# Storing the last 128-token tile of an attention and feed-forward kernel in two DMAs per half instead of four

## The chip, the core and the metric

The kernel runs on one core of a Trainium2 chip. The metric is the device time of one execution in microseconds (us). Before the change it is 646.36 us, the median of 3 runs, which lie between 646.31 and 646.38.

A core has five engines with instruction streams of their own: TensorE (PE, with its weight loads as PEld), VectorE (DVE), ScalarE (ACT), GpSimd (POOL) and SyncE (SP). SP and ACT also start DMAs, each on a hardware queue of its own; the profile calls the issuing instructions SPq and ACTq and the two queues q1 (SP's) and q10 (ACT's). Both queues are served by the same 16 DMA engines. A DMA moves its data in packets, here one packet for each run of contiguous bytes, and reports its end with packets of 4 bytes that count up a semaphore.

## The reference

Eight batches of eight heads with 576 tokens of 64 dimensions go through an attention over 32 memory slots per head. The result, 4608 tokens by 512, goes through a two-layer network with a leaky activation.

```python
a = softmax(phi)                                   # 8, 8, 576, 32
k_m = einsum('bhsm,bhsd->bhmd', a, k)
v_m = einsum('bhsm,bhsd->bhmd', a, v)
x = softmax(q @ k_m.T / 8) @ v_m                   # to (4608, 512)
h = x @ w_in                                       # 512 -> 2048
return maximum(0.01 * h, h) @ w_out                # 2048 -> 512, float32
```

## The kernel before

The order of all work is written out by hand: two long strings of step names (`OPENING`, `LATER`) are run one after the other, and no scheduler moves an instruction. The feed-forward part works on groups of tokens. A group from number 3 on takes 256 tokens, and the last group (number 16) only the 128 that are left, all from the last batch.

For that last group the product with `w_out` is accumulated in two halves of 256 output columns, in two PSUM tiles (`po`). `down_tile` (L1542) issues the matmuls: steps `d55.0` to `d55.3` finish half 0, then comes `end.0`, then `d55.4` to `d55.7` finish half 1, and `end.1` is the last step of the program. Both `end` steps are `store_half`: it scales the finished half into `obs` (half 0 on ACT at L1379, half 1 on DVE at L1377) and sends it to `out` in DRAM.

The tokens of a batch stand permuted in the kernel: column `32 * j + x` of a batch is token `18 * x + j`. The last 128 columns are `j` = 14 to 17 with `x` = 0 to 31. So 32 partitions of `obs` hold one `j`, and go to 32 rows of `out` that lie 18 rows (36 KB) apart, in each a run of 256 floats (1 KB). `store_half` sends one `j` per DMA: `y` = 0 and 2 on SP's queue, 1 and 3 on ACT's. `send` (L1366) does the same for whole rows of the other groups, all on SP.

Each DMA gets one of eight semaphores in turn, `DMAHW0` to `DMAHW7`, and waits until the DMA that had it before has ended. After the last step, SP waits at the end of the program (L1698) for every semaphore, and a barrier of all engines closes the execution.

Of the kernel before, what the change touches and what calls it, by code (L numbers as in the profile page):

```python
# [186 lines left out]
def kernel(  # L187
# [41 lines left out]
    nc = tc.nc  # L229
# [4 lines left out]
    P = 128  # L234
# [1097 lines left out]
    def columns(G, t):  # L1332

        if G < G2:
            for x in range(t * P, (t + 1) * P, 32):
                b, tb = blocks(G)[x // SB]
                y = x % SB // 32
                if b == 0:
                    j = y // 2 * 2 + x // SB if G == 0 else NJ + (0, 2, 1)[y // 2]
                    yield b, j * D + y % 2 * 32  # L1340
                else:
                    yield b, tb * SB + y * 32
        else:
            x0 = 2 * S + (G - G2) * 2 * HT + t * P
            for x in range(x0, x0 + P, 32):
                yield x // S, x % S

    def row_scale(G, t):
        bs = [b for b, _ in columns(G, t)]
        if G == 0:  # L1350
            return 1.0 / WT
        if bs[0] == bs[-1]:
            return osc[:, bs[0]:bs[0] + 1]
        return osc_t[:, bs[0] // 2:bs[0] // 2 + 1]
# [18 lines left out]
    def store_half(G, h, po):  # L1373

        ob, cs = obs[:, h * E:h * E + EH], slice(h * EH, (h + 1) * EH)
        if h:
            nc.vector.tensor_scalar_mul(ob, po[:, 0:EH], row_scale(G, 0))  # L1377
        else:
            nc.scalar.activation(ob, po[:, 0:EH], AF.Copy, scale=row_scale(G, 0))  # L1379
        rows = out.rearrange("(b x j) e -> b j x e", b=B, j=JT)  # L1380
        b, x0 = next(columns(G, 0))
        for y in range(P // 32):
            eng = nc.scalar if y % 2 else nc.sync
            eng.dma_start(rows[b, x0 // 32 + y, :, cs], ob[32 * y:32 * y + 32])

    pos = {}

# [272 lines left out]
    for h in range(2):  # L1660
        steps[f"end.{h}"] = lambda h=h: store_half(G, h, pos[G][h])
# [41 lines left out]
```

## Time and profile before

| | |
|---|---|
| median of 3 runs | 646.36 us (646.31 to 646.38) |
| span of the profiled execution, first to last instruction | 643.4 us |
| median less that span | 2.96 us |
| PE busy | 634.6 us, 99% of the span |
| DVE, ACT busy | 513.4 us, 394.2 us |
| TensorE's clock as granted | full speed in all 40 slices |
| DMA, mean | 95 GB/s |
| stores of the last tile (L1384) | 4 DMAs of 32 KB on SP's queue, 4 on ACT's |

The times are those of one profiled execution, in us from the start of its span. The profile has no device time of its own for that execution, so the 2.96 us between its span and the median of the runs are taken as lying outside the span and as fixed.

### The profile page before, as it was taken

The page shows a single profiled execution, that of the slowest core. Times are in us where ns is not written, and L with a number is a line of the kernel's source. Part 1 is how long each engine was busy: PE and PEld are TensorE (multiplying, and loading weights), DVE is VectorE, ACT ScalarE, POOL GpSimd, SP SyncE. Part 2 cuts the span into 40 slices and gives each one's busy share as a digit, 9 for nine tenths or more (in the row PEclk, how much of TensorE's full clock was granted, in tenths as well). Part 3 has the DMA queues.
Part 4 walks back from the last instruction along what each step waited for, and adds up shares of the span by engine and source line. Part 5 has one row for each costly group of instructions (what it writes and reads, how often), then busy time and mean ns, then how long its engine had stood idle before and what let it go on. Part 6 is the DMA issues. An engine that isn't in the chain of part 4 may idle for free.

```text
span 643.4 us, 16918 instructions
## 1 busy us (share of the span) xinstructions
PE 634.6 (99%) x7149; PEld 481.7 (75%) x7149; DVE 513.4 (80%) x861; ACT 394.2 (61%) x683; POOL 30.0 (5%) x46
## 2 busy tenths in 40 slices
PE   8999999999999999999999999999999999999997
PEld 4545445665546788888888888888888888889896
DVE  5776899998987899899879966799887897574641
ACT  3898987764554556467556665655574576565553
POOL 0000121000010001002000010000010001000000
PEclk9999999999999999999999999999999999999999
DMA  9998632214602645422272001254114101010102
GB/s 323 345 382 274 240 111 54 79 27 86 197 10 36 135 148 85 133 78 42 34 171 91 21 13 44 39 108 148 37 31 80 23 18 34 2 34 2 34 2 50
DMA packets 85884, 61.15 MB, mean 95 GB/s; under 512 B 62128, under 2 KB 69040, under 8 KB 85808
## 3 DMA queue, kind: packets, MB, share of 16 engines
q1 hardware_dynamic: 85328, 59.64, 33.0%
q8 instruction: 56, 0.92, 0.6%
q10 hardware_dynamic: 480, 0.43, 0.2%
q14 instruction: 20, 0.16, 0.1%
HBM read 50.59 MB, written 9.45 MB: 93 GB/s over the span
## 4 chain that ended last, share of the span: by engine, by line
PE 93%; DMA 4%; ACT 1%; DVE 1%; issue 0%; SPq 0%; ACTq 0%
PE po L1507 32%; PE ph L1439 22%; PE po L1396 15%; PE ph L1309 8%; PE ph L1507 5%; PE pa L1217 4%; PE pa L774 3%; DMA arena<-in_moe_w_in_dram 2%; PE po L1542 1%; PE pa L1024 1%; DMA arena<-in_moe_w_out_dram 1%; DMA wo<-in_k_dram 1%; ACT wi L424 0%; PE pa L357 0%; SPq L389 0%
## 5 line engine op out<-in xcount | busy, mean ns | idle before, releaser
L1507 PEld LDWEIGHTS <-arena 128*128 128x128 f16 x2184 | 209.7, 98 | 32.0 <-issue 8.6
L1455 ACT ACTIVATE wi<-ph,g_sc 128x256 f32<-128x256 f32 (+1 forms) x224 | 98.8, 464 | 161.3 <-PE ph L1439 154.3
L1439 PE MATMUL ph<-a,w_mem 128*128 128x256 f16 (+3 forms) x1440 | 144.9, 246 | 0.0
L1439 PEld LDWEIGHTS <-w_mem 128*128 128x128 f16 x1440 | 114.4, 98 | 13.9 <-issue 2.9
L1507 PE MATMUL po<-wo,arena 128*128 128x256 f16 x936 | 122.1, 273 | 0.0
L1507 PE MATMUL po<-arena 128*128 128x256 f16 x936 | 122.1, 273 | 0.0
L1396 PE MATMUL po<-wo,arena 128*128 128x512 f16 (+1 forms) x384 | 110.3, 434 | 0.0
L1484 DVE TENSOR_TENSOR arena<-arena 128x1024 f16<-128x1024 f32 x52 | 63.6, 1222 | 20.6 <-ACT arena L1480 20.6
L1484 DVE TENSOR_TENSOR arena<-wi,arena 128x768 f16<-128x768 f32 (+1 forms) x60 | 54.7, 911 | 10.1 <-ACT arena L1480 10.1
L1476 DVE TENSOR_TENSOR arena<-wi 128x256 f32<-128x256 f32 x104 | 40.4, 430 | 25.9 <-ACT wi L1455 25.3
L1480 ACT CAST arena<-arena 128x1024 f16<-128x1024 f32 x52 | 54.4, 1046 | 8.6 <-DVE arena L1476 8.5
L1309 PE MATMUL ph<-a,w_mem 128*128 128x192 f16 (+2 forms) x304 | 52.1, 317 | 0.0
L1396 PEld LDWEIGHTS <-arena 128*128 128x128 f16 x288 | 27.8, 98 | 29.7 <-issue 0.6
L1480 ACT CAST arena<-wi 128x768 f16<-128x768 f32 (+1 forms) x60 | 46.5, 776 | 1.5
L1476 DVE TENSOR_TENSOR arena<-wi,arena 128x256 f32<-128x256 f32 x104 | 45.7, 440 | 1.8
L1507 PE MATMUL ph<-wo,arena 128*128 128x256 f16 x312 | 42.6, 273 | 0.0
L1182 POOL TENSOR_TENSOR a<-t,a 128x128 f16<-128x128 f32 (+3 forms) x17 | 21.7, 1297 | 444.9 <-ACT a L1177 444.9
L1396 PEld LDWEIGHTS po<-wo,arena 128*128 128x128 f32 x96 | 17.7, 191 | 20.4 <-issue 17.6
L1217 PE MATMUL pa<-wi,vT 64*32 64x512 f16 (+1 forms) x704 | 29.4, 420 | 0.2 <-DVE t L1098 0.2
L1309 PEld LDWEIGHTS <-w_mem 128*128 128x128 f16 x240 | 20.8, 98 | 10.6 <-issue 3.9
L1316 ACT ACTIVATE arena<-ph,g_sc 128x384 f32<-128x384 f32 x32 | 18.3, 579 | 16.1 <-PE ph L1309 15.8
L1250 ACT ACTIVATE w_mem<-pa 128x512 f16<-128x512 f32 x40 | 22.7, 596 | 8.4 <-PE pa L1217 7.4
(233 smaller groups left out, 759.2 us busy)
## 6 DMA issues: line engine op xcount, KB each, us to landing
out_dram<-obs SPq DMA_DIRECT2D x140, 64.0 KB, 1.7
arena<-in_k_dram SPq DMA_DIRECT2D x28, 288.0 KB, 4.4
arena<-in_v_dram SPq DMA_DIRECT2D x28, 288.0 KB, 4.7
arena<-in_q_dram SPq DMA_DIRECT2D x96, 72.0 KB, 2.9
arena<-in_moe_w_in_dram SPq DMA_DIRECT2D x12, 512.0 KB, 7.4
arena<-in_moe_w_out_dram SPq DMA_DIRECT2D x8, 768.0 KB, 7.9
arena<-in_phi_dram SPq DMA_DIRECT2D x7, 576.0 KB, 4.7
arena<-in_moe_w_in_dram SPq DMA_DIRECT2D x8, 256.0 KB, 6.2
```

The lines of the kernel that those rows point to most:

```text
L774: nc.tensor.matmul(var["pk"][g][hh * M:(hh + 1) * M, cs], ld["phi"][rows, hh, j, :], ld["kv", hh][rows, kinds[0]:kinds[-1] + 1, j, :], sta ...
L1182: nc.gpsimd.tensor_tensor(piece(lo, tb), piece(t2, tb), piece(hi, tb), ALU.subtract)
L1217: nc.tensor.matmul(pf[g][cols, :], lhs, rhs, start=(n == 0), stop=(n == len(passes) - 1), tile_position=(g * D, hh * M),)
L1250: nc.scalar.activation(tiles(halves(w16(b, j), g)[:, 0]), w(g), AF.Copy, scale=ws)
L1309: nc.tensor.matmul(ph[:, t0:t0 + n * SB], lhs, rhs, start=(m == 0), stop=(m == len(seq) - 1))
L1396: nc.tensor.matmul(po, lhs, rhs, start=(f == 0 and m == 0), stop=(f == NQ * NF - 1 and m == len(seq) - 1),)
L1439: nc.tensor.matmul(ph[:, t0:t0 + n], lhs, rhs, start=(m == 0), stop=(m == len(seq) - 1))
L1455: nc.scalar.activation(dst, ph, AF.Prelu, scale=g_sc2[:, j:j + 1], alpha=SLOPE)
L1476: nc.vector.tensor_tensor(gt[:, x], y, z, op)
L1480: nc.scalar.copy(dst[:, 0], src)
L1484: nc.vector.tensor_tensor(dst[:, 1], src, dst[:, 0], ALU.subtract)
L1507: nc.tensor.matmul(acc, g[:, x, s, u], rhs, start=(h == 0 and j == 0 and u == 0 and m == 0), stop=(j == NQ - 1 and u == 1 and m == 2), ski ...
```

## The change

`store_half` sends two neighbouring `j` in one DMA. The loop over `y` takes steps of two, the source is 64 partitions of `obs`, and the target is a pattern with two dimensions of rows: 2 values of `j` outside, 32 of `x` inside. SP's queue gets `j` = 14 and 15, ACT's 16 and 17.

```diff
         b, x0 = next(columns(G, 0))
-        for y in range(P // 32):
-            eng = nc.scalar if y % 2 else nc.sync
-            eng.dma_start(rows[b, x0 // 32 + y, :, cs], ob[32 * y:32 * y + 32])
+        for y in range(0, P // 32, 2):
+            eng = nc.scalar if y else nc.sync
+            j = x0 // 32 + y
+            eng.dma_start(rows[b, j:j + 2, :, cs], ob[32 * y:32 * y + 64])
```

On SP the end of the program reads as follows, before (-) and after (+). `obs` is the tile of scaled results, `32x256` and `2x32x256` are rows by elements at the target in DRAM.

```order
 L1366 DMA out_dram<-obs 32x512 [waits DMAHW1_49]
 L1366 DMA out_dram<-obs 32x512 [waits DMAHW2_49]
-L1384 DMA out_dram<-obs 32x256 [waits DMAHW4_49,Activation_49]
-L1384 DMA out_dram<-obs 32x256 [waits DMAHW5_49]
-L1384 DMA out_dram<-obs 32x256 [waits DMAHW7_49,DVE_49]
-L1384 DMA out_dram<-obs 32x256 [waits DMAHW1_49]
-L1698 UNCONDITIONAL_BRANCH
+L1385 DMA out_dram<-obs 2x32x256 [waits DMAHW4_49,Activation_49]
+L1385 DMA out_dram<-obs 2x32x256 [waits DMAHW6_49,DVE_49]
+L1699 UNCONDITIONAL_BRANCH
```

SP issues two DMAs fewer; its second store now waits for DVE's scaling, as the third did before.

On ACT the last rows of the program before are these.

```order
L1379 ACTIVATE obs<-po,osc 128x256 [waits DMAHW2_49,DMAHW1_49,DMAHW7_49,DMAHW0_49,PE_49]
L1384 DMA out_dram<-obs 32x256 [waits DMAHW3_49,Activation_49]
L1384 DMA out_dram<-obs 32x256 [waits DMAHW6_49]
L1384 DMA out_dram<-obs 32x256 [waits DVE_49]
L1384 DMA out_dram<-obs 32x256
```

After the change the same place holds these.

```order
L1379 ACTIVATE obs<-po,osc 128x256 [waits DMAHW2_49,DMAHW1_49,DMAHW7_49,DMAHW0_49,PE_49]
L1385 DMA out_dram<-obs 2x32x256 [waits DMAHW3_49,Activation_49]
L1385 DMA out_dram<-obs 2x32x256 [waits DMAHW5_49,DVE_49]
```

ACT too issues two DMAs fewer, and nothing on any engine stands in another order than before.

## Rows read from the trace of the kernel before

**Rows 1.** The page: busy time of PE, and the chain that ended last by engine.
```profile
PE 634.6 (99%) x7149; PEld 481.7 (75%) x7149; DVE 513.4 (80%) x861; ACT 394.2 (61%) x683; POOL 30.0 (5%) x46
...
PE 93%; DMA 4%; ACT 1%; DVE 1%; issue 0%; SPq 0%; ACTq 0%
```

**Rows 2.** The chain in order of time, its last pieces: start, us, what.
```profile
633.33 5.91 PE po L1542 x54
639.24 0.03 issue
639.26 0.48 DVE obs L1377
```

**Rows 3.** Timeline, four short windows at the end: start, us, engine, line, what.
```profile
637.96 0.47 ACT L1379 ACTIVATE obs<-po,osc 128x256 f32<-128x256 f32 x1 [3.78 <-PE po L1542]
...
638.45 0.31 SPq L1384 DMA_DIRECT2D out_dram<-obs  x1
638.46 0.38 ACTq L1384 DMA_DIRECT2D out_dram<-obs  x1
...
639.77 0.31 SPq L1384 DMA_DIRECT2D out_dram<-obs  x1
639.78 0.37 ACTq L1384 DMA_DIRECT2D out_dram<-obs  x1
...
640.13 0.42 SPq L1384 DMA_DIRECT2D out_dram<-obs  x1
640.18 0.44 ACTq L1384 DMA_DIRECT2D out_dram<-obs  x1
```

**Rows 4.** DMA issues at 639.77 and 639.78: KB, us from issue to landing.
```profile
out_dram<-obs SPq DMA_DIRECT2D x1, 32.0 KB, 1.4
out_dram<-obs ACTq DMA_DIRECT2D x1, 32.0 KB, 1.6
```

**Rows 5.** DMA issue at 640.18: KB, us from issue to landing.
```profile
out_dram<-obs ACTq DMA_DIRECT2D x1, 32.0 KB, 1.7
```

**Rows 6.** SP's waits at the program's end: ns min/median/max, first and last start.
```profile
L1698 SPq EVENT_SEMAPHORE  x7: 17/28/1329, 640.6 to 643.3; - x7
```

**Rows 7.** DMA activity from 638.4 to 641.9 in 40 slices of 0.0875 us.
```profile
DMA  0000000002588414686200000587613687200000
...
DMA packets 384, 0.26 MB, mean 75 GB/s; under 512 B 128, under 2 KB 384, under 8 KB 384
...
q1 hardware_dynamic: 192, 0.13, 14.7%
```

**Rows 8.** Issue times by line: ns min/median/max, first and last start.
```profile
L1384 SPq DMA_DIRECT2D out_dram<-obs x4: 314/368/422, 638.5 to 640.1; - x4
...
L664 SPq DMA_DIRECT2D r1k<-d_mx x12: 487/554/2362, 116.9 to 464.7; - x12
...
L601 SPq DMA_DIRECT2D arena<-in_q_dram x96: 565/630/1811, 138.8 to 497.1; - x96
```

**Rows 9.** Two DMAs of 64 rows: timeline, then DMA activity from 222.4 in slices of 0.05 us.
```profile
222.45 1.13 SPq L664 DMA_DIRECT2D r1k<-d_mx  x2
...
DMA  0000000000000000000000000029333222221213
```

**Rows 10.** SP's DMA queue from 138 to 156: packets; then the DMAs issued there.
```profile
q1 hardware_dynamic: 10000, 1.77, 52.5%
...
arena<-in_q_dram SPq DMA_DIRECT2D x16, 72.0 KB, 2.9
arena<-in_phi_dram SPq DMA_DIRECT2D x1, 576.0 KB, 4.2
```

**Rows 11.** Busy time from 8 to 18 us, with the DMA engines' share and rate at the end.
```profile
core 0: us, PE busy (x) PEld busy (x) DVE busy (x) ACT busy (x) POOL busy (x), PEclk, DMA share, GB/s
8.00:18.00 10.00, 8.63 (x127) 5.52 (x128) 6.92 (x19) 6.14 (x13) 0.00 (x0) 1.00 1.04 388
```

## The prediction

> **What bounds the kernel now.** I read the page first: PE is busy for 99% of the span and the chain that ended last is PE's for 93% [rows 1]. The stores of the last tile are none of that, except at the very end. So I went to the chain in order of time. Its last piece of PE ends at 639.24, DVE scales half 1 until 639.74, and there the chain of engines stops [rows 2]; the span goes on to 643.4. What fills those 3.7 us is in the timeline: half 1 is issued in two rounds on both queues, at 639.77 and 639.78, then at 640.13 and 640.18 [rows 3]. The last of the four lands 1.7 us after 640.18, at about 641.9 [rows 5]. That it is this landing which is waited for shows at the program's end: SP's longest wait starts at 640.6 and takes 1.33, so it ends at 641.93 [rows 6]. The remaining 1.47 us are the closing barrier and stay. Only a change of 641.93 counts.
>
> Half 0 is off the path today. Its DMAs go out at 638.45 and 638.46 and 0.4 later [rows 3], and the activity of the DMA engines shows them over well before half 1 begins: one burst from slice 9 to slice 19 (639.2 to 640.1), then nothing, then half 1 from slice 25 to slice 34 (640.6 to 641.46) [rows 7]. From the last data at 641.46 to 641.93 pass 0.47 us, the landing of the last write.
>
> **What is removed.** The second issue on each queue, which today starts 0.36 to 0.40 after the first [rows 3]. The first DMAs of half 1 land after 1.4 and 1.6 [rows 4], so if nothing else changed, the end would be set by ACT's issue at 639.78.
>
> **What is added: a dearer form.** The new DMAs have 64 partitions on one side and 2 by 32 rows on the other. The plain stores of 32 rows take 0.31 to 0.42 to issue on SP. Two other lines of this program are dearer: L664, with 64 rows of 1 KB, at 0.49 at least and 0.55 in the median, and L601, whose target is 32 partitions of 18 runs while its source is one list of 576, at 0.63 in the median [rows 8]. L601 is the only one with a different number of dimensions on its two sides, like the new store. Between 64 runs and 576 the issue grows by 0.08 in the median, so it is paid for the form and not for the runs. From L664's issue at 222.45 to the first activity (slice 26, 223.70 or a little after) pass 1.28 us [rows 9]; for today's stores it is 639.25 less 638.45, or 0.80 [rows 3, 7]. Bounds for issue to first packet: 0.80, if the form costs nothing, and 1.42, L664's with the 0.14 that L601 takes longer to issue than L664's shortest. I take L664's 1.28, nearest in bytes and rows. So half 0's first packet goes from 639.25 to 639.73.
>
> **What is added: fewer DMA engines, perhaps.** Today each of the eight DMAs writes 16 packets of 4 bytes beside its 32 packets of data: 384 packets, of which 128 are small [rows 7]. So each is shared by all 16 engines, two rows for each. The same holds for every form I could count: from 138 to 156 SP's queue carries sixteen L601 DMAs and one of phi (128 partitions by 4 runs), and 16 x 576 + 512 packets of data leave 272 of the 10000, which is 17 x 16 [rows 10]. With 18 and 4 as inner counts, the share can't be cut along the inner dimension, since 16 divides neither; it follows the outer one (576 and 32, 128 and 128), or the flat list of runs. The new store is the first DMA whose outer count on one side isn't a multiple of 16: it is 2. If the share follows the outer counts, two engines get 32 rows each. And both queues' DMAs go to the same two, if engines are counted from the first. [...]
>
> [...]
>
> **The sum for two engines.** Half 0 brings 32 packets from SP's queue and 32 from ACT's to each of the two engines, half 1 as many: 128 packets of 1 KB each, one after the other. Half 1 is issued at 639.77, its packets are ready by 641.05 (1.28 later), and half 0 is not through by then, so the engines don't pause. The price of a packet lies between two rows. When all engines are saturated with long rows, 388 GB/s over 16 engines at a share of 1.04 is 23.3 GB/s for one, or 44 ns for 1 KB [rows 11]. In today's tail, 14.7% of 16 engines over 3.5 us is 8.23 us for 128 rows on q1, small packets included, so at most 64 ns [rows 7]; there 16 engines at once read the same 32 partitions. Two engines alone are nearer to the first; I take 48. Then 128 x 48 is 6.14 us, from 639.73 to 645.87, and with 0.47 for the landing 646.34. That is 4.41 later than 641.93. On the profiled execution it gives a span of 647.8, and with the 2.96 between span and median 650.8.
>
> Half 0, free today because it ends before half 1 begins, now stands in front of it: that is 3.07 of the 4.41. Bounds: 639.25 + 128 x 44 + 0.47 = 645.35, or 649.8; and 639.87 + 128 x 64 + 0.47 = 648.53, or 653.0. No instruction is queued behind the new DMAs but the closing waits; which of them the last semaphore stands in is worth under 0.1. The new wait of SP and ACT for another semaphore's old DMA is over long before DVE is done at 639.74.
>
> **The rivals.** The measurement can tell some 0.2%, or 1.3 us, from no change.
>
> *All 16 engines share, and the form is dearer.* The first packet comes 0.48 later, and each engine has two packets more per DMA, 2 x 64 ns. ACT's DMA lands 1.6 + 0.48 + 0.13 = 2.21 after 639.78, at 641.99: 0.06 later than today, 646.4. What the second issue cost is paid for the form. Bounds from 645.9 (the form costs nothing) to 646.8 (L601's issue, and double crowding). Not slower. For it: every DMA counted has used 16.
>
> *The change pays.* 16 engines, and no dearer form: 639.78 + 1.6 + 0.13 is 641.51, a gain of 0.42, 645.9. This too is within 0.2%. A gain over 1.3 us would need half 1 to land within 0.9 us of its issue, and 1.4 is the least that a store took here [rows 4]. Against it: both lines of a like form are dearer [rows 8].
>
> *One issue stalls.* Single issues of the dearer forms took 1.81 and 2.36 [rows 8], 1.2 to 1.8 above the median. With 16 engines, one such stall in half 1 gives 647.6 to 648.2.
>
> **How the numbers follow.** Two engines 0.86, since only the cut along outer counts fits both the small packets and the flat price of the issue; 16 engines with the dearer form 0.10, the gain 0.03, a stall 0.01. I predict 650.8. The range 649.6 to 653.0 takes in the bounds of the first case and 0.2 below, and holds nearly all of it, over 8 in 10. Slower by over 0.2%: 0.86 and the stall's 0.01; the same: 0.12; faster: 0.01.
>
> **What would show it.** After the change, the queue q10 should carry 132 packets in the tail, 4 of them small, instead of 192; the DMA engines should be at a level of about an eighth (2 of 16) in an unbroken stretch of some 6 us; the second DMA on each queue should land 6 to 7 us after its issue; issues should take 0.5 to 0.65; SP's last wait should be some 5.5 us. Wrong would be: 160 packets on q10, 32 of them small, in bursts of under 1 us for each half (16 engines), or an unbroken stretch of 3 us, which would mean that the queues use different engines, or four.

## The result, and the profile after

The changed kernel takes 650.99 us (median of 6 runs, 649.09 to 652.39), and the kernel before, run beside it, 646.34 (6 runs, 645.35 to 647.06). The ratio is 1.0065, with a 95% interval of 1.0050 to 1.0079: slower by 4.65 us.

The tail in the timeline of the changed kernel, put together from three windows, in columns as before (start, us, engine, line):

```profile
638.72 0.48 ACT L1379 ACTIVATE obs<-po,osc 128x256 f32<-128x256 f32 x1 [3.78 <-PE po L1543]
639.22 0.65 SPq L1385 DMA_DIRECT2D out_dram<-obs  x1
639.22 1.35 ACTq L1385 DMA_DIRECT2D out_dram<-obs  x1
...
640.03 0.48 DVE L1377 TENSOR_SCALAR obs<-po,osc 128x256 f32<-128x256 f32 x1 [4.63 <-PE po L1543]
640.54 0.54 SPq L1385 DMA_DIRECT2D out_dram<-obs  x1
640.67 0.52 ACTq L1385 DMA_DIRECT2D out_dram<-obs  x1
```

Each queue has two issues where it had four, and each of them takes longer than the plain ones [rows 3]. DVE ends at 640.51, and the span now goes on to 648.6. The DMA activity of the same kernel from 638 to 648, in slices of 0.25 us, shows why:

```profile
DMA  0000000000101111101111111111111111100000
GB/s 0 0 0 0 0 0 0 0 0 4 20 8 49 33 37 12 29 16 45 49 49 49 49 45 45 49 49 49 49 49 49 45 49 45 49 25 0 0 0 0
DMA packets 264, 0.26 MB, mean 26 GB/s; under 512 B 8, under 2 KB 264, under 8 KB 264
...
q1 hardware_dynamic: 132, 0.13, 4.8%
q10 hardware_dynamic: 132, 0.13, 3.7%
```

Where the kernel before had two short bursts at up to 0.8 of the engines [rows 7], there is one stretch from the slice at 640.25 to 647 at a level of 1, which goes with an eighth of 16 engines, thin in its first two microseconds. Of the small packets there are 8 in place of 128: two for each of four DMAs. SP's waits from 639 on (us in total, times, longest) show that the end hangs on it:

```profile
SPq L1699 <- DMA out_dram<-obs: 6.1, 2, 3.5
```

At the program's end SP waits twice for stores, 6.1 us in all; before, its longest wait was 1.33 [rows 6].

One number must be read with care. PE's last product ends at 639.24 before [rows 2] and at 640.00 after, 0.8 apart, with no change ahead of it, and over all profiles of this study it lies between 639.2 and 642.4. So the kernels are compared below by the stretch from the end of DVE's scaling to the end of the span: 3.63 us before (639.75 to 643.38) and 8.12 after, 4.49 more.

### The profile page after: what moved, and what is told of

It reads as the page before. It is cut to its first block, busy times and chain, and to the rows that moved or that the text cites. A ratio compares the mean times of both kernels' runs of the same rounds, so it can differ in the third digit from the quotient of the medians.

```text
span 648.6 us, 16915 instructions
## 1 busy us (share of the span) xinstructions
PE 635.2 (98%) x7149; PEld 482.3 (74%) x7149; DVE 513.5 (79%) x861; ACT 394.5 (61%) x683; POOL 30.0 (5%) x46
## 4 chain that ended last, share of the span: by engine, by line
PE 91%; DMA 4%; SPq 1%; DVE 1%; ACT 1%; issue 0%; DVEq 0%; ACTq 0%
PE po L1508 31%; PE ph L1440 22%; PE po L1397 15%; PE ph L1309 8%; PE ph L1508 5%; PE pa L1217 4%; PE pa L774 3%; PE po L1543 1%; DMA arena<-in_q_dram 1%; PE pa L1024 1%; DMA arena<-in_moe_w_out_dram 1%; DMA arena<-in_moe_w_in_dram 1%; SPq L601 1%; DMA wo<-in_k_dram 1%; ACT wi L424 0%
```

## The experiments

All change only the stores of the last tile, except where the text says more. The edits are shown against the kernel before, those of `e5_one_pitch` and `e7_one_queue` against the changed one; where only added lines are shown for `e2_four_outer`, `e8_32_by_4` and `e6_128_rows`, they take the place of the loop over `y`. Two stretches are given for each: the "tail" is the one just named, and "landing" is from the first issue of half 1 to the last write as the semaphores count it. The small packets of a DMA are taken, as in the prediction, for the number of engines that share it; no row names the engine of a packet. The kernel before had medians of 646.67 (27 runs) beside e1, e2, e3 and e5 and 646.77 (21 runs) beside the others, 0.3 to 0.4 more than the 646.36 from which the expected times were reckoned.

| kernel | DMAs per half, rows at the target | small packets per DMA | landing | tail | median | ratio, 95% interval |
|---|---|---|---|---|---|---|
| before | 4 of 32 | 16 | 2.14 | 3.63 | 646.36 | |
| after | 2 of 2x32 | 2 | 6.73 | 8.12 | 650.99 | 1.0065, 1.0050 to 1.0079 |
| e1_sixteen_outer | 2 of 16x4 | 16 | 2.21 | 3.62 | 647.45 | 1.0010, 0.9998 to 1.0021 |
| e2_four_outer | 1 of 4x32 | 4 | 3.73 | 5.18 | 647.62 | 1.0020, 1.0007 to 1.0032 |
| e8_32_by_4 | 1 of 32x4 | 16 | 2.10 | 3.56 | 647.11 | 1.0001, 0.9981 to 1.0020 |
| e3_half1_only | 4 of 32, then 2 of 2x32 | 16, 2 | 5.11 | 6.48 | 649.39 | 1.0041, 1.0028 to 1.0054 |
| e4_half0_only | 2 of 2x32, then 4 of 32 | 2, 16 | 4.56 | 5.93 | 648.74 | 1.0035, 1.0022 to 1.0047 |
| e5_one_pitch | 2 of 64 | 16 | 2.23 | 3.62 | 646.47 | 0.9995, 0.9984 to 1.0007 |
| e6_128_rows | 1 of 128 | 16 | 1.72 | 3.17 | 646.46 | 0.9997, 0.9988 to 1.0007 |
| e7_one_queue | 2 of 2x32, SP alone | 2 | 6.89 | 8.22 | 651.74 | 1.0081, 1.0066 to 1.0096 |

**Is it the outer count, or the two-dimensional form?** The theory of the prediction is that a DMA is dealt to the engines by its outer counts. The rival is that the form with different dimensions on its two sides goes to two engines whatever it counts. `e1_sixteen_outer` has ACT's leaky activation write the last group's columns x-major, so that 64 partitions are 16 `x` by 4 `j`:

```diff
-            dst, ph = st["gf"][:, i * HT:(i + 1) * HT], ph[:, 0:HT]
+            dst = st["gf"][:, i * HT:(i + 1) * HT].rearrange("p (x j) -> p j x", j=4)
+            ph = ph[:, 0:HT].rearrange("p (j x) -> p j x", j=4)
...
-        for y in range(P // 32):
-            eng = nc.scalar if y % 2 else nc.sync
-            eng.dma_start(rows[b, x0 // 32 + y, :, cs], ob[32 * y:32 * y + 32])
+        for y in range(2):
+            eng = nc.scalar if y else nc.sync
+            j, x = x0 // 32, 16 * y
+            eng.dma_start(
+                rows[b, j:j + 4, x:x + 16, cs].rearrange("j x e -> x j e"), ob[64 * y:64 * y + 64]
+            )
```

> Columns of the last tile are stored x-major (ACT's leaky activation writes them in that order), so that two DMAs per half of 64 rows each, with the same dearer form, count 16 by 4 rows at the target and 64 at the source. If the share follows the outer counts, all 16 engines share: 160 packets on q10 in the tail with 32 small ones, two bursts under 1 us, second issues landing after 2.0 to 2.2 us, time 646.4 (645.9 to 646.8). If the two-dimensional form itself goes to two engines, whatever its outer count: 132 packets on q10, an unbroken stretch of some 6 us, 650.8.

Its DMA activity from 639 to 649:

```profile
DMA  0000000000017600057100000010000000000000
...
q1 hardware_dynamic: 160, 0.13, 3.9%
q10 hardware_dynamic: 160, 0.13, 3.9%
...
out_dram<-obs SPq DMA_DIRECT2D x2, 64.0 KB, 2.0
out_dram<-obs ACTq DMA_DIRECT2D x2, 64.0 KB, 2.2
```

Two short bursts and 160 packets on each queue, 16 small ones for each DMA. The bytes, the queues and the number of DMAs are those of the changed kernel, and so is the kind of pattern; the counts are 16 by 4 and not 2 by 32, and the loss is gone from the tail. The rival falls. Nor can it be where the rows lie in DRAM, 2 KB apart in groups of four here and 36 KB apart in the changed kernel: `e5_one_pitch`, below, also writes rows 36 KB apart, with 16 small packets per DMA and a tail of 3.62. (The median of 647.45 is above the expected range, with an interval that holds 1; whether the strided writes of the activation cost something ahead of the tail isn't settled by it.)

`e2_four_outer` and `e8_32_by_4` make it a pair with nothing else between them but the columns' order: one DMA of all 128 rows on SP, counted 4 by 32 or 32 by 4.

```diff
+        j = x0 // 32
+        nc.sync.dma_start(rows[b, j:j + 4, :, cs], ob)
```

> One DMA of all 128 rows per half, on SP alone, 4 by 32 rows at the target. If the share follows the outer counts, 4 engines: 264 packets on q1 in the tail with 8 small ones, 32 packets per engine and half, landing of half 1 at 643.0 to 644.0, time 647.4 to 648.4. If the form goes to two engines: 260 packets, 128 per engine, 650.8 or later.

`e8_32_by_4` has the activation of `e1_sixteen_outer` and this store:

```diff
+        j = x0 // 32
+        nc.sync.dma_start(rows[b, j:j + 4, :, cs].rearrange("j x e -> x j e"), ob)
```

> As e2_four_outer, one DMA of 128 rows per half on SP, but with the columns x-major, so that the target counts 32 by 4 and not 4 by 32. If the share follows the outer count: 16 engines, 288 packets of which 32 small, landing 2.1 to 2.3 after the issue, stretch from DVE's scaling to the end 3.6 to 3.8 (e2: 5.2), time as the kernel before within 0.2%. If 128 rows in one mixed DMA are slow whatever the order: 264 packets and 5.2.

From 639 to 649, the first with 4 by 32:

```profile
GB/s 0 0 0 0 0 0 0 0 0 0 0 0 20 37 49 98 94 94 98 82 61 82 74 98 90 57 12 0 0 0 0 0 0 33 0 0 0 0 0 0
...
q1 hardware_dynamic: 264, 0.26, 8.6%
```

The same with 32 by 4:

```profile
GB/s 0 0 0 0 0 0 0 0 0 0 0 0 0 0 0 143 332 49 0 0 123 340 62 0 0 0 0 0 0 0 33 0 0 0 0 0 0 0 0 0
...
q1 hardware_dynamic: 288, 0.26, 7.7%
```

With 4 outside there are 8 small packets for two DMAs and a plateau of 98 GB/s; with 32 there are 32 small ones, and each half is over within 0.75 us. With the inner count at 32 in both, 4 outside give four small packets per DMA and the changed kernel's 2 outside give two, with a plateau of 49 GB/s. The rate goes with the engines: up to 24.5 GB/s for each, or 42 ns for 1 KB.

**Do both queues use the same two engines?** `e7_one_queue` puts all four DMAs on SP:

```diff
         for y in range(0, P // 32, 2):
-            eng = nc.scalar if y else nc.sync
             j = x0 // 32 + y
-            eng.dma_start(rows[b, j:j + 2, :, cs], ob[32 * y:32 * y + 64])
+            nc.sync.dma_start(rows[b, j:j + 2, :, cs], ob[32 * y:32 * y + 64])
```

> As after, but all four DMAs on SP's queue. If the two queues of after use the same two engines: 128 packets per engine as there, 2 engines busy for 5.5 to 6.5 us, stretch from DVE's scaling to the end 7.2 to 8.2 us (after: 8.13), the low end if the slow first packets came from two queues at once. If each queue had two engines of its own, or the queue's own order were what costs: clearly longer than after, 10 us or more.

It is no slower in its tail than two queues by more than 0.1 us (8.22, just above the expected 8.2, against 8.12). The changed kernel's trace shows the same from inside. From 643.2 to 643.9 only ACT's queue is served:

```profile
DMA packets 32, 0.03 MB, mean 47 GB/s; under 512 B 0, under 2 KB 32, under 8 KB 32
...
q10 hardware_dynamic: 32, 0.03, 13.1%
```

From 644.9 to 645.9 both are, at the same rate in all:

```profile
DMA packets 46, 0.05 MB, mean 47 GB/s; under 512 B 0, under 2 KB 46, under 8 KB 46
...
q10 hardware_dynamic: 24, 0.02, 6.9%
q1 hardware_dynamic: 22, 0.02, 6.3%
```

A second queue adds nothing to 47 GB/s, so the two share their two engines. Earlier, from 640.2 to 642.6, only SP's queue is served:

```profile
DMA packets 57, 0.06 MB, mean 24 GB/s; under 512 B 0, under 2 KB 57, under 8 KB 57
...
q1 hardware_dynamic: 57, 0.06, 11.6%
```

ACT's first packet starts at 642.68, 3.46 us after its issue at 639.22.

**Which half costs what?** `e3_half1_only` sends half 0 as before and half 1 as after; `e4_half0_only` has the condition the other way round (`if not h`).

```diff
+        if h:
+            for y in range(0, P // 32, 2):
+                eng = nc.scalar if y else nc.sync
+                j = x0 // 32 + y
+                eng.dma_start(rows[b, j:j + 2, :, cs], ob[32 * y:32 * y + 64])
+            return
         for y in range(P // 32):
```

> Half 0 leaves in four DMAs as before, half 1 in two as after. If half 0 standing in front of half 1 on two engines is most of the loss: 64 packets per engine from 641.05 at 44 ns, landing at 644.3 after a scaling that ends at 639.74, time 648.8 (up to 649.8 if the first packets of a stream are slow). If the loss is that of half 1's own DMAs: as after, 650.8.

> Half 0 leaves in two DMAs as after, half 1 in four of 32 rows as before. If half 0 clogs two of the sixteen engines and half 1's rows on those two stand behind it: the two engines are at it until 2.7 to 3.7 us after half 0's first packet, half 1's eight packets on each follow, its last landing comes 1.5 to 2.6 us later than before after the same scaling, time 648.2 to 649.3. If half 1's small shares overtake half 0's, or half 0 uses other engines: the stretch from DVE's scaling to the end is as before, 646.7 (the median that the kernel before had beside the last four).

Against before, half 1 alone lengthens the tail by 2.85 us and half 0 alone by 2.30; both together by 4.49. `e3_half1_only` lies between its two cases: its 649.39 is inside the bound of 649.8, but half 0 in front is 1.64 of the 4.49 (8.12 less 6.48) and not most of it. `e4_half0_only` came out as its first case says. That half 0, which was done before half 1 began, delays half 1's plain DMAs at all shows in the landing times of `e4_half0_only` (KB, us from issue to landing):

```profile
out_dram<-obs SPq DMA_DIRECT2D x2, 32.0 KB, 4.0
out_dram<-obs ACTq DMA_DIRECT2D x2, 32.0 KB, 4.1
```

The plain stores of 32 rows land after 4.0 to 4.1 in place of 1.4 to 1.7 [rows 4, 5]. The small packets show what holds them: the first row is the stretch from 641 to 643, the second from 643 to 644.3.

```profile
DMA packets 242, 0.19 MB, mean 94 GB/s; under 512 B 58, under 2 KB 242, under 8 KB 242
DMA packets 62, 0.05 MB, mean 41 GB/s; under 512 B 10, under 2 KB 62, under 8 KB 62
```

Of the 68 small packets (four plain DMAs with 16, half 0's two with 2), 58 are out by 643, and ten come late, at a rate near that of two engines. That fits 14 of the 16 engines being done early, and each plain DMA waiting for the shares that stand on the two clogged engines, two rows on each, behind half 0's.

**What would two DMAs per half be worth with all engines?** `e5_one_pitch` gives its DMAs a single dimension of 64 rows, 36 KB apart through the batches; the first 32 rows of each (not the second, as the expectation has it) land in batch 6, and the other 32 in the places of the first, so no row of the tile lands in its own place.

```diff
+        rows = out.rearrange("(x j) e -> j x e", j=JT)
         for y in range(0, P // 32, 2):
             eng = nc.scalar if y else nc.sync
-            j = x0 // 32 + y
-            eng.dma_start(rows[b, j:j + 2, :, cs], ob[32 * y:32 * y + 64])
+            j, x = x0 // 32 + y, 32 * (b - 1)
+            eng.dma_start(rows[j, x:x + 64, cs], ob[32 * y:32 * y + 64])
```

> Two DMAs per half of 64 rows, each with one dimension of rows (the second 32 rows of each DMA go to batch 6 in place of their own). 16 engines and the cheap form. If only the sharing and the form cost time: issues of 0.31 to 0.38, 160 packets on q10, landing 1.5 to 1.75 after an issue at 639.78, time 645.9 (645.7 to 646.1). If a DMA of 64 rows is slower in itself than two of 32: 646.3 or more.

`e6_128_rows` does the same with one DMA of 128 rows per half, of which 96 go to batches 4 to 6 and the rest to the places of others.

```diff
+        rows = out.rearrange("(x j) e -> j x e", j=JT)
+        j, x = x0 // 32, 32 * (b - 3)
+        nc.sync.dma_start(rows[j, x:x + 128, cs], ob)
```

> One DMA of 128 rows per half on SP alone, one dimension of rows 36 KB apart (so 96 of its rows go to batches 4 to 6). If 64 partitions make the issue dear and not the number of DMAs or dimensions: issue 0.31 to 0.34, 16 engines, landing 1.7 to 1.9 after the issue, the stretch from the end of DVE's scaling to the end 3.2 to 3.4 us where before has 3.64. If every DMA larger than 32 rows is dear here: issue 0.54 or more, landing 2.2 or later, 3.7 or more.

The issue times by line (ns min/median/max, first and last start), first with 64 rows:

```profile
L1386 SPq DMA_DIRECT2D out_dram<-obs x2: 502/521/540, 639.0 to 640.3; - x2
L1386 ACTq DMA_DIRECT2D out_dram<-obs x2: 502/532/563, 639.0 to 640.3; - x2
```

Then with 128 rows:

```profile
L1384 SPq DMA_DIRECT2D out_dram<-obs x2: 350/350/351, 639.4 to 640.7; - x2
```

My expectation for 64 rows was wrong: with one dimension on both sides they are as dear to issue as 16 by 4 (0.55 to 0.63), and the tail doesn't gain. 128 rows are cheap again, and there the tail gains 0.46 us. In the medians neither can be told from no change.

## Why the prediction was right

**The engines.** The step that decides, the cut along the outer count, held as put: 132 packets on q10 with 4 small ones, an eighth of the engines in one stretch, both queues on the same two. Two engines, the same two for both queues, are a term of the sum that no run had shown when it was made: no row of before has a DMA with fewer than 16 small packets. What the runs then showed are 2, 4, 16 and 16 small packets per DMA for targets of 2 by 32, 4 by 32, 16 by 4 and 32 by 4, and 47 GB/s with one queue as with both. Which two of the 16 they are no row shows. The trace of before could only say that no inner count mattered, and that only if the shares are equal, which I assumed. The second reason, the flat price of the issue (0.55 for 64 runs, 0.63 for 576 [rows 8]), has lost its weight: the issue is dear for 64 rows in one dimension too (0.50 to 0.56 in `e5_one_pitch`), and no run ties its price to the way a DMA is shared. So the trace of before gave no reason of weight against the flat list of runs, which its counts left open; the experiments decide it.

**The dearer form.** Its price was right and its cause wrong. Half 0's first packet comes 1.25 after the issue (1.28 predicted, from L664), and half 1's issues take 0.52 and 0.54. But it is not the different dimensions of the two sides: `e5_one_pitch` has one dimension on both and takes 0.50 to 0.56. L664, the row I took as nearest, also has 64 rows. Not foreseen: ACT's first issue took 1.35, which the stream hides.

**The stream.** 128 packets per engine were to take 6.14 us at 48 ns; from 640.47 to 646.94 they took 6.47, or 50.5 on average, at 42 to 43 in the steady part (48 GB/s on average from 642.5 to 646.5) and much more at the beginning. That 48 ns came near is in part luck: the steady price is below the lower bound of 44, which would make some 5.5 us, and the slow beginning, which the sum did not have, adds about 1 us. The landing of the last write took 0.33 in place of 0.47, and the end of the program 1.36 in place of 1.47; what shortened the two isn't shown. SP's last wait was put at 5.5 and is 6.1, in two pieces. In all the tail is 4.49 longer against 4.41.

**Half 0 in front.** Here a sentence was wrong. I put half 0 down for 3.07 of the 4.41. That is the length of its packets, not the delay, because 1.3 us of them go out before half 1 could start. Taking half 0's share away (`e3_half1_only`) gives back 1.64 of 4.49.

**The time outside the span.** I took 2.96 us as fixed. The profiled execution after has 650.43 with a span of 648.6, so 1.8, and the other profiles of the study read the same (649.82 with 648.0). By that the profiled execution of before took about 645.2, just below the lowest of its kernel's runs beside the changed one (645.35). The forecast didn't suffer, because it added the difference of two tails to the median, and the span that it named, 647.8, was too short by 0.8, what PE's last product came later.

**The rivals.** With 16 engines the first rival's price was right: 0.06 later by its sum, and 0.01 and 0.07 less in the tails of `e1_sixteen_outer` and `e8_32_by_4`. A gain like its 0.42 was seen only with a cheap issue (0.46 in `e6_128_rows`, with one DMA of 128 rows in place of two of 64).

## What to carry to other kernels

Count the small semaphore packets, or the level of the DMA engines, behind every DMA whose pattern has been reshaped: fewer DMAs can mean fewer engines (here 2 small packets per DMA where the four DMAs had 16 each, and a tail of 8.12 in place of 3.63). Where a pattern has a small count and a large one, try it with the small one inside: 16 by 4 and 32 by 4 at the target kept 16 small packets and tails of 3.62 and 3.56, 2 by 32 and 4 by 32 had 2 and 4, and tails of 8.12 and 5.18. Other counts weren't tried. A store that was off the path can come onto it when it hasn't drained before the last one starts (half 0 alone cost the tail 2.30 in `e4_half0_only`), so a transfer in the tail is priced with all that shares its engines.

## What had not been expected of the hardware

The stream into two engines starts slowly. In the changed kernel the first packet starts at 640.47; the seven slices from 640.5 to 642.25 move 27 GB/s on average, and the plateau is 49. It isn't two queues that are served at once, for only SP's has packets there, and a slow beginning stands with one queue in `e7_one_queue` too, from 639 to 649:

```profile
GB/s 0 0 0 0 0 0 0 0 16 12 16 45 45 29 33 33 41 20 29 37 49 49 45 45 49 49 49 49 45 45 49 49 49 45 25 0 0 0 0 0
```

What it is stays open. ACT's issue took 1.35 to 1.37 in the three cases in which SP issued for the same two engines at almost the same time (both at 639.22 in the changed kernel, at 641.57 and 641.58 in `e3_half1_only`, both at 639.0 in `e4_half0_only`), and 0.63 at most when 16 engines share; in the changed kernel ACT's first packet starts 3.46 us after that issue. This too is only observed. And a store of 64 partitions takes 0.50 to 0.56 to issue where 32 take 0.31 to 0.44 and 128 take 0.35, all with one dimension of rows.
